# A two-layer long-convolution and SwiGLU kernel: a new hand-written order, searched with another charge for a held GpSimd instruction

## The chip, the cores and the metric

The kernel runs on one core of one Trainium2 chip. The metric is the device time of one execution in microseconds, as the median of several runs. The engines are named as in the profile: PE (TensorE), with PEld its weight loads, DVE (VectorE), ACT (ScalarE), POOL (GpSimd) and SP (SyncE, which here only issues transfers).

## The reference

Two layers, each a gated long convolution with a residual, and then a SwiGLU feed-forward block with a residual, on 2048 rows of 512 columns in bf16. Both layers use the same weights.

```python
x = A_q                                              # 2048 x 512
for layer in (0, 1):                                 # written out twice in the reference
    x = x + conv_block(layernorm(x), A_k, A_v, A_shift_k, A_ssm_k, A_ssm_D)
    x = x + ffn(layernorm(x), B_w_gate, B_w_up, B_w_down)

def conv_block(q, k, v, shift_k, ssm_k, ssm_D):
    k_shift = sum over 4 taps t of k shifted down by 3 - t rows, times shift_k[:, 3 - t]
    kv = k_shift * v
    y = irfft(rfft(kv padded to 4096) * rfft(ssm_k padded to 4096))[:2048]
    return q * (y + kv * ssm_D)

def ffn(x, w_gate, w_up, w_down):                    # 512 -> 1792 -> 512
    return (silu(x @ w_gate) * (x @ w_up)) @ w_down
```

The convolution's result y depends only on k, v and the filter, so both layers use the same y, and only the layer norms, the products with q and the feed-forward blocks differ between them.

## The kernel before, in words

The rows are cut into four chunks of 512 rows (NB = 4) and each chunk into two halves of 256 rows. A half in one layer is a unit (layer, chunk, half). The convolution is done chunk by chunk as matmuls with cosine and sine tables (`fwd` and `inv`): the spectra X (of kv) and G, H (of the filter) come out of TensorE into PSUM, are evicted to SBUF mostly by ScalarE, are multiplied on VectorE (tiles `t`, `Z`, `m`), and go through TensorE again to give `Yk`.

A unit's feed-forward block takes the normalised rows, transposed as `zT` (by a transposing transfer from SyncE's queue, for the first half by TensorE), multiplies them with the gate and up weights into PSUM tiles `pf`, which ScalarE evicts (`sg` with silu, `hr` or `ht` as a copy); VectorE multiplies the two; in groups handled by rows the product `hr` is transposed by a transfer into `sg`, and TensorE multiplies it with the down weights into `pd`. Some groups use a seven-product scheme instead (`cb`, `ps7`, evicted as `mt`).

A layer norm takes the mean and variance of a row either on VectorE (`bn_stats`, `bn_aggr` into `mv`, columns of constants in `bst` appended) or on ScalarE (sums by `jk`, with `nm` and then `ve`), and then needs (variance + eps) to the power -0.5. That power is a tiny GpSimd instruction, 128 x 2 elements, written to `rstd` (`power`, line 905 of the profile): after `mv` or after `ve`. VectorE or ScalarE then normalises with `rstd`, in some cases through `nmr` = -mean * rstd.

Every piece of work is registered with `add` as an operation with its engine, a cost, and its reads and writes: 1716 operations, of which 523 are TensorE's, 488 ScalarE's, 512 VectorE's, 150 SyncE's and 43 GpSimd's. `ORDER` is a table of 1716 ranks: the nth number is the place of the nth registered operation in one global list. `Plan.order` sorts by it and `Plan.walk` goes through the list with a timing model, which chooses the slot of each ring buffer. `Plan.issue` then emits the operations in the list's order. Each engine therefore executes its own operations in the list's order, and waits across engines are made by semaphores that follow from the reads and writes. The model's times are not on the chip; what reaches it are the order on each engine, the ring slots, and where the fixed number of 33 warm-up matmuls go at the start.

In the model a power whose input ports are taken by VectorE is held: `pend` is the pending power and `held` the time until which VectorE's back-to-back SBUF-to-SBUF operations keep it. It is settled when an operation that needs it is reached, when VectorE leaves a hole, or when the next GpSimd operation in the list is reached.

The operations that the steps below touch are: `ve` (operation 107), the first power (108), `nmr` (109), the two memsets of `bst` (2 and 3, lines 1276 and 1277), the squares `jk` (105 and 106), the evictions of X (line 525, operations 132, 135, 116, 119, 147, 141, 138, 144), the products `t` and `Z` (lines 748 and 752), the first normalised `z` (line 964) and the transfers into `zT` (line 994) and `sg` (line 1132).

Of the kernel before, what the change touches and what calls it, by code (L numbers as in the profile page):

```python
# [149 lines left out]
class Plan:  # L150
# [79 lines left out]
    def walk(self, seq, loads):  # L230
# [6 lines left out]
        def settle(g):  # L237
            pend.end = max(pend.start + pend.cost, g + pend.cost - 0.08)
            t["POOL"] = max(t["POOL"], pend.end)
# [1289 lines left out]
```

## Time and profile before

| what | before |
|---|---|
| median of 3 runs | 339.8 us (339.25 to 340.37) |
| the profiled execution's own time | 339.51 us |
| its span, first to last instruction | 337.7 us |
| granted TensorE clock | 1.00 |
| PE busy | 330.9 us, 98% |
| DVE busy | 299.9 us, 89% |
| ACT busy | 262.8 us, 78% |
| POOL busy | 35.4 us, 10%, in 48 instructions |

Matmuls are pipelined and their ends are modelled, so a busy PE is not PE at its peak, and a few per cent of the matmuls' records are missing (2141 matmuls against 2172 weight loads). In an answer of the timeline a row gives start, duration, engine, line, operation, tiles, count, and in brackets the idle time of the engine just before it with what ended it. In an answer of the waits a row gives the waiting instruction, what it waited for, the total in us, the number of times and the longest. The time outside the span (1.8 us) has no instruction in it.

### The profile page before, as it was taken

Reading aid. Unit: us, or ns where it says so; the run is one execution under the profiler, and the core shown is the slowest. Engines: PE = TensorE matmul, PEld = TensorE weight load, DVE = VectorE, ACT = ScalarE, POOL = GpSimd, SP = SyncE. Lnnn points to the kernel's source line nnn. Section 1 sums busy time; section 2 is a strip of 40 time slices with the busy share of each in tenths; the row PEclk is TensorE's granted clock in tenths of the full one; section 3 lists DMA queues with packets and bytes.
Section 4 is the critical chain, followed back from the end, with each engine's and each line's share of the span. In section 5 each row is a group of like instructions: output and inputs, shape, how many; then the busy total and the mean of one; then the engine's idle time right before and its main releaser. Section 6 shows DMA issues by size and latency. Waiting matters only on the chain.

```text
span 337.7 us, 5898 instructions
## 1 busy us (share of the span) xinstructions
PE 330.9 (98%) x2141; PEld 204.6 (61%) x2172; DVE 299.9 (89%) x512; ACT 262.8 (78%) x534; POOL 35.4 (10%) x48
## 2 busy tenths in 40 slices
PE   9999999999999999999999999999999999999996
PEld 7655864645445564745454464744455687858884
DVE  8899999999888998999999999999999787877545
ACT  7889999999967466999899894999675556475462
POOL 4050001102100000122010100011100100100000
PEclk9999999999999999999999999999999999999999
DMA  7999604632346147421324434510514230204101
GB/s 255 350 229 376 130 13 66 151 82 41 71 93 94 36 91 188 95 49 32 62 53 106 97 60 110 138 35 16 96 28 82 56 72 17 48 18 93 49 3 62
DMA packets 77993, 31.59 MB, mean 94 GB/s; under 512 B 69766, under 2 KB 75787, under 8 KB 77963
## 3 DMA queue, kind: packets, MB, share of 16 engines
q1 hardware_dynamic: 77808, 31.13, 39.6%
q8 instruction: 17, 0.28, 0.4%
q14 instruction: 14, 0.11, 0.1%
q10 hardware_dynamic: 154, 0.07, 0.1%
HBM read 12.33 MB, written 2.10 MB: 43 GB/s over the span
## 4 chain that ended last, share of the span: by engine, by line
PE 91%; ACT 4%; DMA 2%; issue 1%; DVE 1%; SPq 1%
PE pf L416 56%; PE pd L1210 20%; PE ps L1085 7%; PE ps L416 6%; DMA kTb<-in_A_k_dram 1%; PE wm L1495 1%; DMA sg<-hr 1%; ACT H L525 1%; SPq L1132 1%; ACT ks L620 1%; ACT n L959 0%; ACT jk L929 0%; DVE t L748 0%; ACT ev L525 0%; ACT hr L1124 0%
## 5 line engine op out<-in xcount | busy, mean ns | idle before, releaser
L416 PEld LDWEIGHTS <-zT 128*128 128x128 bf16 x528 | 51.6, 98 | 58.5 <-DMA zT<-z 0.2
L416 PE MATMUL pf<-wg_sb,zT 128*128 128x512 bf16 x255 | 64.3, 379 | 0.5
L416 PE MATMUL pf<-wu_sb,zT 128*128 128x512 bf16 x260 | 64.3, 379 | 0.2
L1210 PE MATMUL pd<-wd_sb,sg 128*128 128x512 bf16 x189 | 48.1, 379 | 0.9 <-DMA sg<-hr 0.3
L1124 ACT CAST hr<-pf 128x512 bf16<-128x512 f32 x66 | 38.4, 593 | 12.4 <-PE pf L416 8.5
L1123 ACT ACTIVATE sg<-pf 128x512 bf16<-128x512 f32 x66 | 38.8, 608 | 11.3 <-PE pf L416 10.2
L416 PE MATMUL pf<-zT,wg_sb 128*128 128x256 bf16 x368 | 46.0, 273 | 0.1
L416 PE MATMUL pf<-zT,wu_sb 128*128 128x256 bf16 x368 | 45.9, 273 | 0.0
L758 DVE TENSOR_TENSOR t<-X,G 128x4096 bf16<-128x4096 bf16 x18 | 40.9, 2284 | 0.1
L416 PEld LDWEIGHTS <-wu_sb 128*128 128x128 bf16 x368 | 36.0, 98 | 8.1
L416 PEld LDWEIGHTS <-wg_sb 128*128 128x128 bf16 x368 | 35.9, 98 | 7.9 <-issue 0.4
L1183 ACT ACTIVATE sg<-pf 128x512 bf16<-128x512 f32 x46 | 27.3, 607 | 10.8 <-PE pf L416 10.8
L1187 ACT CAST ht<-pf 128x512 bf16<-128x512 f32 x46 | 26.8, 595 | 9.8 <-PE pf L416 8.0
L905 POOL TENSOR_TENSOR rstd<-mv,nhalf 128x2 f32<-128x2 f32 x20 | 17.0, 852 | 158.2 <-DVE mv L915 134.7
L1210 PEld LDWEIGHTS <-sg 128*128 128x128 bf16 x200 | 19.5, 98 | 21.7 <-DMA sg<-hr 0.8
L1210 PE MATMUL pd<-wd_sb,ht 128*128 128x512 bf16 (+1 forms) x124 | 29.7, 369 | 0.1
L914 DVE BATCH_NORM_STATS2 bst<-xc 128x6 f32<-128x512 bf16 x40 | 26.5, 683 | 0.5
L905 POOL TENSOR_TENSOR rstd<-ve,nhalf 128x2 f32<-128x2 f32 x12 | 14.6, 1218 | 111.7 <-ACT ve L942 111.7
L1190 DVE TENSOR_TENSOR ht<-ht,sg 128x512 bf16<-128x512 bf16 (+1 forms) x31 | 16.6, 544 | 8.8 <-ACT sg L1183 4.5
L1130 DVE TENSOR_TENSOR hr<-hr,sg 128x1024 bf16<-128x1024 bf16 x27 | 18.4, 682 | 4.2 <-ACT sg L1123 2.0
L1210 PEld LDWEIGHTS <-ht 128*128 128x128 bf16 x126 | 12.3, 98 | 13.1 <-DVE ht L1190 0.3
L525 ACT ACTIVATE X<-ps 128x512 bf16<-128x512 f32 x32 | 18.4, 604 | 1.6 <-PE ps L416 0.9
(143 smaller groups left out, 522.1 us busy)
## 6 DMA issues: line engine op xcount, KB each, us to landing
hn<-in_A_ssm_k_dram SPq DMA_DIRECT2D x4, 512.0 KB, 3.7
vt<-in_A_v_dram SPq DMA_DIRECT2D x4, 512.0 KB, 5.5
xc<-in_A_q_dram SPq DMA_DIRECT2D x4, 512.0 KB, 5.6
out_dram<-xc SPq DMA_DIRECT2D x15, 128.0 KB, 1.9
wg_sb<-in_B_w_gate_dram SPq DMA_DIRECT2D x1, 1792.0 KB
wu_sb<-in_B_w_up_dram SPq DMA_DIRECT2D x1, 1792.0 KB, 8.9
wd_sb<-in_B_w_down_dram SPq DMA_DIRECT2D x1, 1280.0 KB, 12.1
sg<-hr SPq DMA_TRANSPOSE x66, 2.4
```

The costliest lines, as they stand in the source:

```text
L416: nc.tensor.matmul(o, lhsT=lhsT, rhs=rhs, start=(n == 0), stop=(n == len(terms) - 1))
L525: add("ACT", act(D), lambda: nc.scalar.activation(out=view(), in_=ps.t[:], func=ACT.Copy, scale=scale), r=[ps], w=[(buf, keys)], conv=conv)
L758: dve(8 * D, lambda t=t, part=part: nc.vector.tensor_mul(out=t.t[:], in0=x.t[:, :, part:part + 1, :].to_broadcast((P, R, 2, D)), in1=g.t[: ...
L905: add("POOL", cost, lambda: nc.gpsimd.tensor_tensor(out=rstd.t[:], in0=var(), in1=nhalf.t[:].to_broadcast((P, n)), op=ALU.pow), r=reads + ...
L914: add("DVE", 0.6, lambda st=st, i=i: nc.vector.bn_stats(out=st.t[:, 0:6], in_=xs[c].t[:, i, :]), r=[(xs[c], (i,))], w=[st])
L1085: nc.tensor.matmul(bank.t[:, half_ * C:(half_ + 1) * C], lhsT=lhsT(i), rhs=rhs(i), start=(first and i == 0 and half_ == 0), stop=(last and ...
L1123: add("ACT", act(D), lambda ps=ps, dst=dst, o=o, which=which: nc.scalar.activation(out=rows(dst, o), in_=ps.t[:], func=ACT.Silu) if which ...
L1124: out=rows(dst, o), in_=ps.t[:], func=ACT.Silu) if which == "g" else nc.scalar.copy(out=rows(dst, o), in_=ps.t[:]),
L1130: dve(n * W, lambda: nc.vector.tensor_mul(out=hr.t[:], in0=hr.t[:], in1=sg.t[:]), [sg], [hr], due=(unit, k / pairs, 0.0, "h"))
L1183: add("ACT", act(D), lambda ps=ps, o=o, sg=sg: nc.scalar.activation(out=sg.t[:, o:o + 2, :], in_=ps.t[:], func=ACT.Silu), r=[ps], w=[(sg, ...
L1187: add("ACT", act(D), lambda ps=ps, o=o, ht=ht: nc.scalar.copy(out=ht.t[:, o:o + 2, :], in_=ps.t[:]), r=[ps], w=[(ht, (o // 2,))], due=(uni ...
L1210: nc.tensor.matmul((pds[o] if not cs.start else pds[HP]).t[:, cs], lhsT=ht.tiles(q, o), rhs=wt["d"].t[:, ft, cs], start=(ft == std0 and no ...
```

## The change

Two things change: one constant of the timing model in `walk`, and the whole table `ORDER`, which was searched anew with that constant. No operation is added, removed or altered.

```diff
 ORDER = [
-    7, 79, 141, 188, 2, 3, 1, 15, 23, 4, 12, 0, 5, 13, 68, 9, 10, 6, 8, 11, 28, 19, 14, 24, 20, 25, 32, 33, 38, 69, 144, 146, 18, 46, 17, 45, 22, 43,
...
+    10, 40, 110, 214, 1, 6, 7, 8, 21, 2, 3, 0, 4, 5, 14, 12, 9, 11, 13, 16, 24, 20, 17, 22, 23, 26, 28, 31, 34, 15, 45, 50, 27, 43, 19, 47, 37, 44,
...
 ]
...
             if pend is not None and (o.eng == "POOL" or pend in o.preds):
-                settle(held if pend.late == 1 or pend in o.preds else max(held, pend.start) + 1.2)
+                settle(held if pend.late == 1 or pend in o.preds else max(held, pend.start) + 4.0)
                 pend = None
```

Read as ranks, the operations of the first layer norm and around it move so:

| operation | rank before | rank after |
|---|---|---|
| memset of bst, first (2) | 141 | 110 |
| memset of bst, second (3) | 188 | 214 |
| second square, jk (106) | 124 | 111 |
| first two X evictions (132, 135) | 111, 117 | 116, 120 |
| ve (107) | 133 | 124 |
| next X evictions (116, 119, 138) | 119, 121, 126 | 126, 129, 151 |
| power, rstd (108) | 134 | 170 |
| last Z product ahead of nmr | 163 (158) | 169 (159) |
| nmr (109) | 165 | 171 |
| first kTb product of the next chunk | 166 (259) | 167 (253) |
| ks evictions (260, 254) | 171, 206 | 183, 191 |

126 rows, old and new, of the table ORDER are left out of this document.

## Prediction

> **What bounds the kernel now.** I read the page first: busy time, clock and the chain that ended last.
>
> ```profile
> span 337.7 us, 5898 instructions
> PE 330.9 (98%) x2141; PEld 204.6 (61%) x2172; DVE 299.9 (89%) x512; ACT 262.8 (78%) x534; POOL 35.4 (10%) x48
> PEclk9999999999999999999999999999999999999999
> PE 91%; ACT 4%; DMA 2%; issue 1%; DVE 1%; SPq 1%
> ```
>
> TensorE is busy for 330.9 of 337.7 us at a full clock, and it carries 91% of the chain. The change leaves every matmul in place; it only moves them. So a new order can win no more than the time in which TensorE stands, and the next view is who TensorE waited for, and then its timeline around those waits.
>
> ```profile
> PE ps L416 <- DMA kTb<-in_A_k_dram: 0.8, 1, 0.8
> PE pd L1210 <- DMA sg<-hr: 0.3, 1, 0.3
> PE ps L416 <- ACT ks L620: 0.2, 1, 0.2
> ...
> 183.88 4.32 PE pf L416 x20
> ...
> 22.76 1.08 PE L416 MATMUL ps<-dg,kTb 128*128 128x128 bf16 x16 [0.82 <-DMA kTb<-in_A_k_dram]
> ...
> 31.27 0.38 PE L416 MATMUL ps<-vt,fwd 128*128 128x512 bf16 x1 [0.21 <-ACT ks L620]
> 31.55 0.72 PE L1022 MATMUL ptz<-ident,z 128*128 128x128 bf16 x8
> 32.33 0.59 PE L416 MATMUL ps<-vt,fwd 128*128 128x512 bf16 x2
> 32.88 0.49 PE L416 MATMUL pf<-zT,wg_sb 128*128 128x256 bf16 x3
> ...
> 241.33 1.04 PE L1210 MATMUL pd<-wd_sb,sg 128*128 128x512 bf16 x4 [0.33 <-DMA sg<-hr]
> 333.19 1.47 PE L1210 MATMUL pd<-wd_sb,ht 128*128 128x256 bf16 x12
> ```
>
> Twenty 512-column matmuls take 4.32 us, so one costs 0.216 us of TensorE's time, although a single one is drawn 0.38 long; a stall is therefore 0.16 us longer than its bracket. Read so, TensorE lost 0.98 us before 22.76 (0.82 + 0.16), 0.37 at 31.27 (0.21 + 0.16), and 0.49 at 241.33 (0.33 + 0.16). From 31.27 to 32.88 pass 1.61 us for three vt matmuls, one whose record is missing (0.86 together) and eight transposes of z at about 0.056: 0.3 lost there too. After 333.19 + 1.47 = 334.66 there is only the tail, to 337.7. Between 32.88 and 334.66 only the 0.49 us is lost: the whole body is full. The pool to win from is 0.98 + 0.37 + 0.3 + 0.49 = 2.1 us, 0.6% of the time; what can be lost is open.
>
> The head (to 32.88) is where the altered charge belongs, so I read VectorE and GpSimd there.
>
> ```profile
> 15.64 1.28 DVE L748 TENSOR_TENSOR t<-X,G 128x1024 bf16<-128x1024 bf16 x2
> 16.96 0.43 DVE L752 TENSOR_TENSOR Z<-t,t 128x512 bf16<-128x512 bf16 x1
> ...
> 20.15 4.36 POOL L905 TENSOR_TENSOR rstd<-ve,nhalf 128x2 f32<-128x2 f32 x1 [13.43 <-ACT ve L942]
> 24.47 0.11 POOL L1276 MEMSET bst<- 128x12 f32 x1
> ...
> 22.52 1.42 DVE L752 TENSOR_TENSOR Z<-t,t 128x512 bf16<-128x512 bf16 x4
> 24.55 0.16 DVE L953 TENSOR_TENSOR nmr<-nm,rstd 128x2 f32<-128x2 f32 x1 [0.61 <-POOL rstd L905]
> 24.63 1.89 DVE L889 TENSOR_TENSOR m<-Z 128x1024 bf16<-128x1024 bf16 x3
> 31.08 0.73 DVE L964 TENSOR_SCALAR z<-xc,mv,rstd 128x512 bf16<-128x512 bf16 x2 [0.25 <-POOL rstd L905]
> ...
> 56.84 0.68 DVE L663 TENSOR_TENSOR X<-m 128x1024 bf16<-128x1024 bf16 x1
> 57.53 0.69 DVE L1130 TENSOR_TENSOR hr<-hr,sg 128x1024 bf16<-128x1024 bf16 x1
> 57.10 0.97 POOL L905 TENSOR_TENSOR rstd<-ve,nhalf 128x2 f32<-128x2 f32 x1 [9.77 <-ACT ve L942]
> 191.46 1.23 POOL L905 TENSOR_TENSOR rstd<-ve,nhalf 128x2 f32<-128x2 f32 x1 [17.00 <-ACT ve L942]
> ```
>
> The first power (rstd of L905) took 4.36 us where others take 0.97 or 1.23. It starts at 20.15 while VectorE runs SBUF-to-SBUF operations without a break, and ends 0.57 after the last of them (22.52 + 1.42 = 23.94). It is also the only one with an unrelated GpSimd instruction, the bst memset, queued behind it. VectorE then idles 0.61 us for it, and from 24.55 VectorE works through to z at 31.08 nearly without a hole. So that 0.61 us sits on the path that sets 32.88.
>
> **The change part by part.** The constant is not on the chip; what changes is the order of each engine and the ring slots. Reading each list position of the two tables as the rank of that operation: of TensorE's 523 entries 445 stand elsewhere, of ScalarE's 488 it is 415, of VectorE's 512 it is 390, of SyncE's 150 it is 105, of GpSimd's 43 it is 16. Costs of the instructions stay, so each goes in at zero by itself; the sum is of waits.
>
> *The first power.* Before, ScalarE computes ve after five X evictions, both squares and the hs copy; after, it comes right after the first two X evictions. One bst memset goes ahead of the power (rank 110 against 170), the other still stands next behind it (rank 214).
>
> ```profile
> 10.42 0.60 ACT L525 ACTIVATE ev<-ps 128x512 bf16<-128x512 f32 x1 [0.67 <-PE ps L416]
> 13.31 1.09 ACT L525 ACTIVATE ev<-ps 128x512 bf16<-128x512 f32 x2 [0.35 <-PE ps L416]
> 14.98 1.08 ACT L525 ACTIVATE X<-ps 128x512 bf16<-128x512 f32 x2
> 16.33 0.60 ACT L525 ACTIVATE X<-ps 128x512 bf16<-128x512 f32 x1 [0.26 <-PE ps L564]
> 19.76 0.31 ACT L942 ACTIVATE ve<-sm,eps 128x2 f32<-128x2 f32 x1
> 23.88 0.59 ACT L620 CAST ks<-ps 128x512 bf16<-128x512 f32 x1 [0.78 <-PE ps L416]
> ```
>
> The second square is moved ahead of the X evictions; the holes of 0.67 and 0.35 us on ScalarE take most of its 0.81, because the table puts the ev matmuls ahead of the kTb ones. So the two X evictions stay at about 14.98, ve runs at 16.0 to 16.3 in a hole that was 0.26, and the power starts at 16.3 instead of 20.15. VectorE's order up to 16.96 is the same, and 14.98 leads to 15.64: at 15.64 + 1.28 = 16.92 it leaves a hole of 0.04 (Z at 16.96 needs the t just written). At 57.52/57.53 a hole of 0.01 was enough: that power ended at 58.07, 0.55 after it. I take it that 0.04 is enough too: rstd is ready near 17.5, seven microseconds before nmr needs it. nmr then follows the last Z without a hole, 0.08 ahead of its drawn end as the m at 24.63 is ahead of nmr's (24.71): 23.86 instead of 24.55, a gain of 0.69. The bounds are 0 (the hold lasts to 23.94 as before, since nmr stands behind the same products) and 0.7; the row at 57.10 is nearest, so 0.69. If ve comes later than 16.9 the cover is gone and the value is 0.
>
> The Trainium skill, page "SBUF — State Buffer", section "SBUF: two separate sides", says that VectorE and GpSimd hold the shared port pair as an exclusive lock for one whole instruction and the loser blocks. The trace agrees for 57.10 and 191.46, but not for 20.15, which was passed over for nine VectorE instructions. By that rule alone the power at 20.15 would have taken about what those two took, the old charge would do, and this part would be worth 0.
>
> *What else is late then.* z moves from 31.08 to about 30.4 if ScalarE and TensorE follow. ScalarE had a hole of 0.78 at 23.88; the table now puts three H evictions there and ks behind. TensorE gets three matmuls more ahead of the kTb ones (3 x 0.216 = 0.65 of the 0.98). One more vt product is put between z and the zT copy, which I take to cost 0.09 (of its 0.33 all but what TensorE's transposes cover). Head: 0.69 - 0.09 = 0.6, with bounds 0 and, if TensorE's stalls up to 32.88 all went, 1.6.
>
> *The body.* Here each hand-over by a transposing DMA is packed tightly, and re-packed by the new table. At 241.33 the distance in matmul time from the last product to its consumer was 5.2 us; in the new table the smallest such distance is 5.6. So the 0.49 there may go; but others shrink (rivals). I set the body's stalls equal, 0.49, bounds 0 and 2.8. *Tail:* the last four down-projection blocks stand in the same sequence, behind 1.7 us of filler for the last silu; 0, with 0.2 either way.
>
> Sum against the profiled execution: 339.5 (337.7 span + 1.8 around it) - 0.6 = 338.9. That execution lies 0.3 under the median of the runs, 339.8, so on the median's scale 339.2.
>
> **The rivals.** *Slower: a transpose that lands late.* The new table has less TensorE work between products and the layer norm's consumer at some units.
>
> ```profile
> 168.15 1.03 PE L416 MATMUL ps<-Z,inv 128*128 128x512 bf16 x4
> 179.15 2.50 SPq L994 DMA_TRANSPOSE zT<-z  x2
> 183.71 1.46 PE L416 MATMUL pf<-wg_sb,zT 128*128 128x512 bf16 x6
> 278.63 0.71 PE L1085 MATMUL ps<-wsa,cb 128*128 128x256 bf16 x5
> 294.67 1.19 SPq L994 DMA_TRANSPOSE zT<-z  x1
> 299.30 1.03 PE L416 MATMUL pf<-wu_sb,zT 128*128 128x512 bf16 x4
> ...
> sg<-hr SPq DMA_TRANSPOSE x66, 2.4
> ```
>
> With 2.4 us from issue to landing, zT issued at 179.15 was there at 181.6 and used at 183.7: 2.1 spare. The tables cut the matmul time from the inverse's product (168.15) to that use from 15.1 to 12.3 us, 2.8 less: 0.7 short. For the one issued at 294.67 (297.1, used 299.3, 2.2 spare) the cut is from 20.1 to 16.7, 3.4 less: 1.2 short. TensorE takes its queue in order, so each shortfall moves the end. Both come to 1.9; with the 0.4 to 0.5 that the other shortened places would add, 2.3: 339.2 + 2.3 = 341.5. For it: those distances, and 0.49 at 241.33 shows that a miss costs what it is late. Against it: the same tables move VectorE and ScalarE work out from between (twelve strangers instead of fifteen on VectorE in the second). It decides the sign once the shortfalls left over exceed 1.6 us.
>
> *No effect at the power.* The memset of rank 214 has nothing to wait for, so it still stands behind the power on the chip; the planner escapes its charge because nmr precedes it in the list. If a follower makes the hold and a 0.04 hole isn't enough, VectorE idles 0.61 at 24.55 as now, and the rest is equal: 339.8.
>
> *Faster.* The head gains 0.6 and the hand-over at 241.33, with 5.6 or more everywhere, no longer stalls: 0.6 + 0.49 = 1.1, giving 338.7.
>
> **How the numbers follow.** A measurement of this kernel can tell about 0.3%, 1.0 us. Forecast (339.2) 0.35, no effect at the power (339.8) 0.10, faster (338.7) 0.24, slower (341.5) 0.31. Same is then 0.45. The range leaves out a full 2.1 us gain and a third late hand-over: 338.3 to 341.7.
>
> **What would show it.** Right: a first power that starts near 16.3 and lasts about 1.2 us, nmr with no idle time before it, the first pf matmul near 32.3, span near 337.1. Wrong in the head: a power of 4 us or more and 0.6 idle before nmr. Wrong in the body: TensorE waits on zT<-z or sg<-hr of more than 0.5 in all between 33 and 334. The prediction fails if those waits exceed 2.5 us, or if the X evictions slip past 15.5 because ScalarE's holes do not take the square.

## The result and the profile after

| | before | after |
|---|---|---|
| median of 18 runs each | 339.57 us (339.25 to 340.37) | 340.56 us (339.83 to 342.45) |
| ratio to before, 95% interval | | 1.0033 [1.0021, 1.0045] |
| profiled execution, its span | 339.51 us, 337.7 us | 341.35 us, 339.6 us |

The new order is slower, by about 1 us, and its runs scatter more (2.6 us from lowest to highest, 1.1 before). The profiled execution of after lies 0.8 us above its median, so its terms are larger than the median's. In one execution, the profiled one of E1, the granted TensorE clock was 0.85 and the time 389.31 us; it enters no ratio, and no view below is of it. The page of after, busy time and chain:

```profile
span 339.6 us, 5922 instructions
PE 334.0 (98%) x2172; PEld 203.9 (60%) x2172; DVE 299.6 (88%) x512; ACT 262.9 (77%) x534; POOL 34.1 (10%) x48
PE 87%; DMA 5%; DVE 4%; SPq 1%; issue 1%; ACT 0%
PE pf L416 54%; PE pd L1210 20%; PE ps L1085 7%; PE ps L416 6%; DMA xc<-in_A_q_dram 4%; DMA kn<-in_A_k_dram 1%; SPq L460 1%; DVE G L687 1%; DVE m L646 1%; DVE t L758 1%; DVE bst L914 1%; DVE H L652 0%; DVE ht L1190 0%; ACT ev L525 0%; SPq L500 0%
```

TensorE's share of the chain fell from 91% to 87%, and 4% now runs through a load, xc<-in_A_q_dram, that the chain of before did not show. The first power and what follows it, from the timeline of after:

```profile
16.09 1.29 DVE L748 TENSOR_TENSOR t<-X,G 128x1024 bf16<-128x1024 bf16 x2
16.79 1.17 POOL L905 TENSOR_TENSOR rstd<-ve,nhalf 128x2 f32<-128x2 f32 x1 [9.79 <-ACT ve L942]
17.41 0.42 DVE L752 TENSOR_TENSOR Z<-t,t 128x512 bf16<-128x512 bf16 x1
...
24.32 0.15 DVE L953 TENSOR_TENSOR nmr<-nm,rstd 128x2 f32<-128x2 f32 x1
32.64 1.03 PE L416 MATMUL pf<-zT,wu_sb 128*128 128x256 bf16 x8
33.51 1.04 PE L416 MATMUL pf<-zT,wg_sb 128*128 128x256 bf16 x8
...
334.62 1.90 PE L1210 MATMUL pd<-wd_sb,ht 128*128 128x512 bf16 x14
```

The power lasts 1.17 us instead of 4.36 and nmr has no idle time before it. From the first t to nmr pass 24.32 - 16.09 = 8.23 us, before 24.55 - 15.64 = 8.91. The first pf matmul is at 32.64 against 32.88. The last group of matmuls ends at 334.62 + 1.90 = 336.52 against 334.66. So the head is 0.24 us shorter, the body 303.88 long against 301.78, 2.10 longer, and the tail the same (3.1 against 3.0). Where the body lost it, first TensorE and ScalarE, then VectorE, from the same timeline:

```profile
42.46 0.38 PE L416 MATMUL ps<-vt,fwd 128*128 128x512 bf16 x1
43.66 1.04 PE L1210 MATMUL pd<-wd_sb,ht 128*128 128x512 bf16 x4 [0.83 <-DVE ht L1190]
45.09 1.03 PE L416 MATMUL pf<-zT,wg_sb 128*128 128x256 bf16 x8 [0.39 <-ACT sg L1183]
45.96 1.04 PE L416 MATMUL pf<-zT,wu_sb 128*128 128x256 bf16 x8
47.03 0.38 PE L416 MATMUL ps<-vt,fwd 128*128 128x512 bf16 x1
...
48.98 0.38 PE L416 MATMUL ps<-vt,fwd 128*128 128x512 bf16 x1
49.52 1.69 PE L1210 MATMUL pd<-wd_sb,ht 128*128 128x512 bf16 x7 [0.16 <-DVE ht L1190]
...
43.04 1.52 ACT L959 ACTIVATE n<-xc,nmr,rstd 128x512 bf16<-128x512 bf16 x2 [1.95 <-DVE nmr L953]
...
32.07 0.42 DVE L1025 COPY zT<-ptz 128x512 bf16<-128x512 bf16 x1
34.98 0.69 DVE L914 BATCH_NORM_STATS2 bst<-xc 128x6 f32<-128x512 bf16 x1 [2.49 <-DMA xc<-in_A_q_dram]
35.59 2.34 DVE L646 TENSOR_TENSOR m<-H 128x2048 bf16<-128x2048 bf16 x2
...
42.92 0.69 DVE L1190 TENSOR_TENSOR ht<-ht,sg 128x1024 bf16<-128x1024 bf16 x1
```

At 0.216 us a 512-column matmul and 0.109 a 256-column one (32.64 to the next group at 33.51 is eight of them), TensorE stood 43.66 - 42.46 - 0.22 = 0.98, then 45.09 - 43.66 - 0.86 = 0.57, 47.03 - 45.96 - 0.87 = 0.20 and 49.52 - 48.98 - 0.22 = 0.32: 2.07 us. The small gaps further on come to 0.45 us and stand against the 0.49 that before lost at 241.33, so these four are nearly all of the body's loss. Each goes back to one place: VectorE stands 2.49 us at the batch-norm statistics of the xc row of chunk 1, which wait for the row's load, and everything behind it comes late: the products of the filter spectrum (m, H, G), nmr, for which ScalarE waits 1.95, and ht at 42.92. The answering rows of before:

```profile
32.31 0.42 DVE L1025 COPY zT<-ptz 128x512 bf16<-128x512 bf16 x1 [0.16 <-PE ptz L1022]
32.65 2.35 DVE L646 TENSOR_TENSOR m<-H 128x2048 bf16<-128x2048 bf16 x2
...
38.71 0.69 DVE L914 BATCH_NORM_STATS2 bst<-xc 128x6 f32<-128x512 bf16 x1
...
40.51 0.68 DVE L1190 TENSOR_TENSOR ht<-ht,sg 128x1024 bf16<-128x1024 bf16 x1
```

There the statistics stood behind the two m, four H and one G product. The load moved too. SyncE's queue in the timeline of before, and the load's row in the DMA view of that stretch (the last column is the time from issue to landing):

```profile
20.41 0.58 SPq L503 DMA_DIRECT2D wu_sb<-in_B_w_up_dram  x1
21.04 0.51 SPq L500 DMA_DIRECT2D wd_sb<-in_B_w_down_dram  x1
21.59 4.26 SPq L492 DMA_DIRECT2D xc<-in_A_q_dram  x1
25.89 0.43 SPq L500 DMA_DIRECT2D wd_sb<-in_B_w_down_dram  x1
```

```profile
xc<-in_A_q_dram SPq DMA_DIRECT2D x1, 512.0 KB, 12.8
```

The same two views of after:

```profile
19.67 0.58 SPq L503 DMA_DIRECT2D wu_sb<-in_B_w_up_dram  x1
20.30 1.13 SPq L500 DMA_DIRECT2D wd_sb<-in_B_w_down_dram  x2
21.47 4.74 SPq L492 DMA_DIRECT2D xc<-in_A_q_dram  x1
```

```profile
xc<-in_A_q_dram SPq DMA_DIRECT2D x1, 512.0 KB, 13.5
```

In after both parts of wd (512 KB and 1280 KB) go ahead of xc, in before only the larger one. Counted from the issue of wu, xc lands 21.59 + 12.8 - 20.41 = 14.0 us later in before and 21.47 + 13.5 - 19.67 = 15.3 in after. So two moves met: the load 1.3 us later in its queue, and its reader 6.3 us earlier on VectorE (38.71 to 32.4).

### The profile page after: what moved, and what is told of

Its sections match the earlier page's. It is cut to its first block, busy times and chain, and to the rows that moved or that the text cites. A ratio compares the mean times of both kernels' runs of the same rounds, so it can differ in the third digit from the quotient of the medians.

```text
span 339.6 us, 5922 instructions
## 1 busy us (share of the span) xinstructions
PE 334.0 (98%) x2172; PEld 203.9 (60%) x2172; DVE 299.6 (88%) x512; ACT 262.9 (77%) x534; POOL 34.1 (10%) x48
## 4 chain that ended last, share of the span: by engine, by line
PE 87%; DMA 5%; DVE 4%; SPq 1%; issue 1%; ACT 0%
PE pf L416 54%; PE pd L1210 20%; PE ps L1085 7%; PE ps L416 6%; DMA xc<-in_A_q_dram 4%; DMA kn<-in_A_k_dram 1%; SPq L460 1%; DVE G L687 1%; DVE m L646 1%; DVE t L758 1%; DVE bst L914 1%; DVE H L652 0%; DVE ht L1190 0%; ACT ev L525 0%; SPq L500 0%
## 5 line engine op out<-in xcount | busy, mean ns | idle before, releaser
L1210 PE MATMUL pd<-wd_sb,sg 128*128 128x512 bf16 x200 | 49.1, 379 | 0.0
L1123 ACT ACTIVATE sg<-pf 128x512 bf16<-128x512 f32 x66 | 38.2, 600 | 13.2 <-PE pf L416 10.8
L416 PE MATMUL pf<-zT,wg_sb 128*128 128x256 bf16 x368 | 46.7, 273 | 0.4 <-ACT sg L1183 0.4
L905 POOL TENSOR_TENSOR rstd<-mv,nhalf 128x2 f32<-128x2 f32 x20 | 18.2, 908 | 157.1 <-DVE mv L915 157.1
L1183 ACT ACTIVATE sg<-pf 128x512 bf16<-128x512 f32 x46 | 26.7, 603 | 8.2 <-PE pf L416 6.8
L905 POOL TENSOR_TENSOR rstd<-ve,nhalf 128x2 f32<-128x2 f32 x12 | 12.1, 1004 | 115.9 <-ACT ve L942 115.9
## 6 DMA issues: line engine op xcount, KB each, us to landing
wd_sb<-in_B_w_down_dram SPq DMA_DIRECT2D x1, 1280.0 KB, 12.8
```

Source lines behind the costliest of these rows:

```text
L416: nc.tensor.matmul(o, lhsT=lhsT, rhs=rhs, start=(n == 0), stop=(n == len(terms) - 1))
L905: add("POOL", cost, lambda: nc.gpsimd.tensor_tensor(out=rstd.t[:], in0=var(), in1=nhalf.t[:].to_broadcast((P, n)), op=ALU.pow), r=reads + ...
L1123: add("ACT", act(D), lambda ps=ps, dst=dst, o=o, which=which: nc.scalar.activation(out=rows(dst, o), in_=ps.t[:], func=ACT.Silu) if which ...
L1183: add("ACT", act(D), lambda ps=ps, o=o, sg=sg: nc.scalar.activation(out=sg.t[:, o:o + 2, :], in_=ps.t[:], func=ACT.Silu), r=[ps], w=[(sg, ...
L1210: nc.tensor.matmul((pds[o] if not cs.start else pds[HP]).t[:, cs], lhsT=ht.tiles(q, o), rhs=wt["d"].t[:, ft, cs], start=(ft == std0 and no ...
```

## The experiments

Theory T puts the loss on VectorE's early reader; R1 on the moved load alone; R2 on the head; R3 on the rest of the new order. All kernels were run beside the kernel before on the same chip, and the ratio is to that. The edits move entries of `ORDER` (E9 also lifts one dependence), and the diffs show one engine's sequence each, with the operation's number in brackets.

**E1: the reader back in its place.**

```diff
 VectorE, kernel after
   zT<-ptz (222)
-  bst<-xc (520)
   m<-H x2, H<-m x4, G<-H,G (251)
+  bst<-xc (520)
   G<-H,G (252)
```

> The kernel after, with one VectorE instruction put back: the batch-norm statistics (bst<-xc) that read the xc row of chunk 1 stand behind the first G product (H,G->G) again, as in the kernel before, instead of right behind the zT copy. Theory T (VectorE stands 2.49 us at that instruction for a load that lands at 34.97, and TensorE loses 2.06 us between 42.5 and 49.5 for it): no wait on xc on VectorE, TensorE stalls between 42 and 50 below 0.5 us, a median 1.0 to 2.0 us below that of after, so near 339.0 where after gave 340.56. Rival R1 (the SyncE move alone, xc issued behind all of wd, is the cost): no change, 340.6. Rival R3 (the loss is spread over re-packed hand-overs): less than 0.5 us gained, the stalls turn up elsewhere.

338.94 us, ratio 0.9985 [0.9976, 0.9994]. One instruction moved takes away the whole loss and some more: T's figure, 339.0, and not R3's; the order of the head (R2) is untouched by this edit. R1 predicted no change and falls in this form. The signs that T named for the profile are there in E10, which has the reader in the same place: no VectorE wait on xc, and no gap on TensorE between 42 and 50 us.

**E2: the load back in its place.**

```diff
 SyncE, kernel after
   wu (79)
-  wd, 512 KB (80)
   wd, 1280 KB (81)
   xc (287)
+  wd, 512 KB (80)
   vt (290)
```

> The kernel after, with one SyncE entry put back: the xc load of chunk 1 goes ahead of the 512 KB part of wd, as in before. VectorE's order is that of after. Theory T: xc lands about 0.6 us sooner (34.4 rather than 34.97), VectorE waits about 1.9 us instead of 2.49, and the median falls by 0.3 to 0.6 us, to about 340.1. R1: the whole loss goes, 339.0 to 339.3. R3: no change.

338.91 us, ratio 0.9981 [0.9972, 0.9990]. T had said 340.1, which was wrong: this move alone also takes the whole loss away. The waits between 31 and 52 us show why:

```profile
DVE bst L914 <- DMA xc<-in_A_q_dram: 0.6, 1, 0.6
```

Issued behind only the larger part, xc landed 13.9 us after the issue of wu; and in this execution wu went out at 18.94 rather than 19.67. VectorE waited 0.56 us, and of that 0.12 reached TensorE (a gap at 47.4). So some 0.4 us of the wait had cover here: what stood behind it could come that much later before TensorE had to stand. R1, which said 339.0 to 339.3 here, gets this one nearly right. So neither fits both runs, and the theory had to be: either move alone fits under the cover, both together do not (theory C).

**E3 and E4: each move alone, in the kernel before.**

```diff
 E3, VectorE, kernel before              E4, SyncE, kernel before
   zT<-ptz (222)                           wu (79)
+  bst<-xc (520)                        +  wd, 512 KB (80)
   m<-H x2, H<-m x4, G<-H,G (251)          wd, 1280 KB (81)
-  bst<-xc (520)                           xc (287)
   G<-H,G (252)                         -  wd, 512 KB (80)
```

> The kernel before, with one VectorE instruction moved: the batch-norm statistics of chunk 1's xc row stand right behind the zT copy, ahead of the products of the filter spectrum, as in after. Theory T: VectorE waits 34.4 - 32.65 = about 1.8 us for xc there, everything behind it is late by that, TensorE stalls 1 to 1.8 us between 40 and 50, median 340.6 to 341.3 where before gave 339.57, with a wider spread. R1 and R3: no change beyond 0.3 us.

> The kernel before, with one SyncE entry moved: the xc load of chunk 1 goes behind both parts of wd, as in after. Theory T: xc lands 0.6 us later or so, about 35.0, and the statistics that read it run at 38.7 as before, so no change: 339.4 to 339.8. R1: 1 us slower or more, 340.6.

E3: 340.02 us (339.41 to 341.27), ratio 1.0010 [0.9999, 1.0021]; E4: 339.77 us, 1.0003 [0.9994, 1.0012]. E4 came as T expected. E3 is at most half of what T expected, and its interval takes in no change. In its profiled execution VectorE waited 0.26 us for xc, since xc landed at 33.36 rather than 34.4, and TensorE lost 0.3 behind it, in three gaps of 0.1 that before does not have. The first of them, 43.39 - 42.41 - 0.87 = 0.11:

```profile
42.41 1.04 PE L416 MATMUL pf<-zT,wg_sb 128*128 128x256 bf16 x8
43.39 1.03 PE L416 MATMUL pf<-zT,wu_sb 128*128 128x256 bf16 x8
```

The others are at 44.36 and 48.15. That fits the 0.4 by which the median lies above that of before.

**E5 and E6: none of the two moves in after, both in before.** E5 has the edits of E1 and E2, E6 those of E3 and E4.

> The kernel after, with both places put back: the statistics of chunk 1's xc row behind the first G product, and the xc load ahead of the 512 KB part of wd. Theory C (the loss is a conjunction: moved behind wd, xc lands 15.0 to 15.3 us after the issue of wu instead of 13.9, and moved ahead of the filter products, its reader waits for it; either one put back removes it): no more than either repair alone gave, 338.9 within 0.2, lowest spread of all, no VectorE wait on xc. Rival: the two costs add, then this gains again about 0.6, 338.3.

> The kernel before, with both moves made, the statistics early and the xc load behind all of wd, and nothing else of the change. Theory C: xc lands 15.2 us after the issue of wu, which came between 18.5 and 20.4, so at 33.7 to 35.6, VectorE reaches its reader at about 32.65 and waits 1.1 to 3.0 us; some 0.5 of it is hidden, the rest reaches TensorE: median 340.3 to 341.2 where the single moves gave 340.02 and 339.77. Rival R3 (the rest of the new order is needed for the loss): no more than the two single moves together, 340.2 or less, and no TensorE stall over 0.3 us between 40 and 50.

E5: 338.95 us (338.68 to 339.33), ratio 0.9980 [0.9972, 0.9989]. E6: 341.0 us (five executions), 1.0043 [1.0030, 1.0055]. Theory C holds on both sides. In before the two moves cost 0.4 and 0.2 us singly, neither clear of the scatter, and 1.4 together; in after they cost nothing singly and 1.6 together (340.56 against 338.95). The waits of E6 between 31 and 52 us are those of after, smaller:

```profile
ACT n L959 <- DVE nmr L953: 1.1, 1, 1.1
DVE bst L914 <- DMA xc<-in_A_q_dram: 1.0, 1, 1.0
```

Its timeline has the loss on TensorE, eight 256-column matmuls and then a gap:

```profile
42.60 1.04 PE L416 MATMUL pf<-zT,wg_sb 128*128 128x256 bf16 x8
44.37 1.03 PE L416 MATMUL pf<-zT,wu_sb 128*128 128x256 bf16 x8 [0.74 <-ACT sg L1183]
```

That gap is 44.37 - 42.60 - 0.87 = 0.90; with two of 0.1 at 45.34 and 49.13 TensorE lost 1.1 us, all of VectorE's 1.04. The VectorE wait and TensorE's loss behind it in the profiled executions are 0.26 and 0.3 (E3), 1.04 and 1.1 (E6) in the order of before, and 0.56 and 0.12 (E2), 2.49 and 2.07 (after) in the new one: in these executions the order of before pays the wait in full, and the new one hides some 0.4 us of it. What in the new order hides them is not shown.

**E9: the early reader with an early load.** VectorE's order is the change's own.

```diff
 SyncE, kernel after
   wu (79)
+  xc (287)
   wd, 512 KB (80)
   wd, 1280 KB (81)
-  xc (287)
 line 1461
-        load_x(c, after=[wd])
+        load_x(c, after=[wu if c == 1 else wd])
```

> The kernel after with VectorE's order as the change has it (statistics of chunk 1's xc row right behind the zT copy), but the xc load directly behind wu, ahead of both parts of wd. In the profiles a 512 KB part ahead of xc delayed its landing by 1.3 us (13.9 to 15.2 after the issue of wu), so 1792 KB less ahead should bring it to about 10.6 after the issue of wu, 29 to 31. Theory C: VectorE, there at 32.3, waits for nothing, TensorE has no stall over 0.3 between 40 and 50, median 338.7 to 339.0, a spread under 1 us: the early place of the statistics costs nothing by itself. Rival (the early statistics cost by holding the filter products up by their own 0.7 us, or wd, landing later, stalls the down-projection at 42): 339.4 or more.

338.86 us, ratio 0.9981 [0.9972, 0.9991]. xc landed 9.6 us after its issue at 19.17, that is 10.2 after the issue of wu, 5.1 sooner than in after. The early place of the statistics costs nothing in this order; only the landing counts. E1, E2, E5, E9 and E10 lie within 0.1 us of one another, and each beats both kernels, before by 0.15 to 0.2%, and after, going by the medians, by 0.5%.

**E7: no GpSimd instruction behind the power.** The altered charge is for a power with a follower, so this takes the follower away.

```diff
 GpSimd, kernel before
+  bst memset (2)
+  bst memset (3)
   rstd<-ve,nhalf (108)
-  bst memset (2)
-  bst memset (3)
```

> The kernel before, with the two bst memsets of GpSimd moved ahead of the first power, so that no other GpSimd instruction stands behind it. It tests what the altered charge says: that a GpSimd instruction that follows holds a power up. Theory F (the follower holds it): the power at 20.2 lasts 1 to 1.3 us instead of 4.36, nmr loses its 0.6 us of idle time, median 339.0. Theory H (only a hole between VectorE's instructions lets it in, follower or not): 4.36 us again, nmr waits 0.6, median 339.4 to 339.8.

339.65 us, ratio 1.0001 [0.9991, 1.0012]. The power and nmr:

```profile
20.95 4.37 POOL L905 TENSOR_TENSOR rstd<-ve,nhalf 128x2 f32<-128x2 f32 x1 [14.14 <-ACT ve L942]
25.35 0.16 DVE L953 TENSOR_TENSOR nmr<-nm,rstd 128x2 f32<-128x2 f32 x1 [0.61 <-POOL rstd L905]
```

Without any follower it lasts 4.37 us, as with it. Theory F falls; the follower does not hold the power.

**E8: only the early power, in before.**

```diff
 ScalarE, kernel before
+  square jk (106)
   X evictions (132, 135)
+  ve (107)
   X evictions (116, 119)
-  square jk (106)
   X eviction (138), hs copy (165)
-  ve (107)
```

> The kernel before, with two ScalarE instructions moved: the second square of the head ahead of the X evictions and ve right behind the first two of them, as in after; everything else as in before, the memsets behind the power too. Prediction's step for the first power: the power starts at 16.3 to 16.8, is let in by the hole of 0.04 us at 16.9, lasts about 1.2, nmr follows the last Z without idle time, gain 0.6, median 339.0. Rival: the X evictions slip by up to 0.8 us behind the square and eat the gain, 339.6.

340.01 us, ratio 1.0012 [1.0003, 1.0020]: slower. The first t of VectorE, the power and nmr:

```profile
17.17 1.29 DVE L748 TENSOR_TENSOR t<-X,G 128x1024 bf16<-128x1024 bf16 x2 [0.73 <-ACT X L525]
17.89 1.15 POOL L905 TENSOR_TENSOR rstd<-ve,nhalf 128x2 f32<-128x2 f32 x1 [11.16 <-ACT ve L942]
25.39 0.16 DVE L953 TENSOR_TENSOR nmr<-nm,rstd 128x2 f32<-128x2 f32 x1
```

The power lasts 1.15 us and nmr does not wait, but the square ahead of the evictions makes VectorE wait 0.73 for X, more than the 0.61 that nmr gave back. That is the rival's case, but the median lies 0.4 above that of before, and this difference gives only 0.1 of it; the rest is not shown. The change has the early power without this price, since in its order the first square runs at 12.55, ahead of two ev evictions, and the second at 14.73, about where before has its first.

**E10 and E11: the power later, in the repaired kernel E5.** ve goes behind the first four X evictions (E10) or behind the hs copy, as in before (E11).

> The repaired kernel (after with statistics and xc load both back in their places), with ve moved on ScalarE from behind the first two X evictions to behind the first four, so that the first power starts after VectorE's hole of 0.04 us at 17.5 to 17.7 instead of before it. Theory H (the power gets in only at a hole of VectorE): it starts near 18.5 and is held to 25.0, 5 us or more, nmr waits 0.6 us, median 0.4 to 0.7 us above the repaired kernel's 338.95, so 339.4 to 339.6. Rival (what matters is which instructions run beside it, a power started at 18.5 takes 1.2 us): no wait before nmr, 338.95.

> The repaired kernel (after with statistics and xc load both back in their places), with ve on ScalarE as late as in before, behind the hs copy, so that the first power starts near 21.2, beside t, m, t, t and four Z of VectorE. Theory Q (a power that starts while a queue of VectorE instructions stands ready is passed over by all of them): it is held to the last Z and 0.58 us beyond, to about 25.2, so it lasts some 4 us, nmr waits 0.6 us, and the median is 0.4 to 0.7 us above the repaired kernel's 338.95, near 339.5. Theory O (it only waits for the instruction that is running, wherever it starts, as at 18.76): 0.6 to 1.3 us, no wait, 338.9.

E10: 338.87 us, ratio 0.9981 [0.9972, 0.9989]; E11: 339.71 us, 0.9999 [0.9989, 1.0009]. The timeline of E10, then of E11:

```profile
18.01 1.29 DVE L748 TENSOR_TENSOR t<-X,G 128x1024 bf16<-128x1024 bf16 x2
18.76 1.11 POOL L905 TENSOR_TENSOR rstd<-ve,nhalf 128x2 f32<-128x2 f32 x1 [11.80 <-ACT ve L942]
19.21 1.09 DVE L752 TENSOR_TENSOR Z<-t,t 128x512 bf16<-128x512 bf16 x3
24.57 0.15 DVE L953 TENSOR_TENSOR nmr<-nm,rstd 128x2 f32<-128x2 f32 x1
```

```profile
21.01 0.69 DVE L889 TENSOR_TENSOR m<-Z 128x1024 bf16<-128x1024 bf16 x1
21.05 3.77 POOL L905 TENSOR_TENSOR rstd<-ve,nhalf 128x2 f32<-128x2 f32 x1 [14.03 <-ACT ve L942]
22.81 1.43 DVE L752 TENSOR_TENSOR Z<-t,t 128x512 bf16<-128x512 bf16 x4
24.85 0.16 DVE L953 TENSOR_TENSOR nmr<-nm,rstd 128x2 f32<-128x2 f32 x1 [0.61 <-POOL rstd L905]
```

E10 refutes theory H: VectorE goes from t to Z without a hole (18.01 + 1.29 = 19.30, Z at 19.21), and the power still ends at 19.87, 0.57 us behind the t that ran when it started. In E11 it starts at 21.05, is passed over by seven VectorE instructions and ends 0.58 us behind the last of them (22.81 + 1.43 = 24.24, against 24.82). That brings the 0.61 us before nmr back and costs 0.76 us in the median against E5, or 0.65 by the two ratios, as the kernel before gave 339.62 beside E5 and 339.76 beside E11.

**E12: which instruction stands beside it.**

```diff
 VectorE, kernel before
   t<-X,G (157)
-  m<-Z (184)
   t<-X,G x3, Z<-t,t x4, nmr (109)
+  m<-Z (184)
   m<-Z x3
```

> The kernel before, with the one m product of VectorE that runs when the first power starts (m<-Z at 20.11) moved behind nmr, to the other three; the power then starts beside t, t, t and four Z. Theory M (the hold comes from the power starting in the m product): the power lasts 1.2 us or less. Theory Q (any ready queue passes it over): it is held to the last Z again, 4.36 - 0.6 = 3.8 us, nmr 0.6 us behind the last Z. The time of the whole says little here, as the first inverse matmuls have to wait for m: 339.5 to 340.6.

339.42 us, ratio 0.9991 [0.9982, 1.0000]. The power lasted 0.72 us. But without m VectorE came to the next t too soon and stood 0.41 us for X, and the power ran in that hole; so M and Q are not told apart.

## Why the prediction was wrong

The forecast was 339.2 us, 0.6 below the 339.8 of the first three runs. It came out as 340.56, 1.0 above the 339.57 of 18 runs: the head gained what was forecast, and the body, set at no change, lost more.

*The first power: right in size, and in part by luck.* It gave 0.69 for VectorE's gain up to nmr; 8.91 - 8.23 is 0.68. The start came at 16.79 rather than 16.3, and the head's gain in the profile is 0.24 rather than 0.6 only because the chain began 0.45 us later in this execution (first t at 16.09 against 15.64); in the chain's own time the first pf came 16.55 us after the first t instead of 17.24. That start is the execution's and not the order's: in E9, which keeps the new head, the first t is at 15.68, in E7, which keeps the old one, at 16.43. E11 put a price on the hold in the whole time, 0.65 to 0.76 us. But the reason given, a hole of 0.04 us that lets the power in before 16.9, was not needed: in E10 a start at 18.76 was as good, and in E11 one at 21.05 was held. E7 shows that the follower, which the changed constant charges for, plays no part. The power at 20.15 was passed over by eight VectorE instructions, the m that ran when it started among them, and not by nine.

*The step that failed is the one before the sum: "Costs of the instructions stay, so each goes in at zero by itself", with the body's stalls then set equal.* SyncE's 105 and VectorE's 390 moved entries were counted and not walked. Only the hand-overs by transposing DMA were measured for their slack; no load was set against its reader. The rows of before had it, as shown above: xc lands at 34.4 and its reader comes at 38.71, 4.3 us of slack. The tables put the reader behind the zT copy, which ends at 32.7, and 512 KB more ahead of the load; the 1.3 us for those is measured, and the profile of before gives 1.4, as its DMA engines moved a mean of 373 GB/s from 26 to 34 us. That is a wait of 34.4 + 1.3 - 32.7 = 3.0 us on VectorE, a loss of up to that, where the sum had 0. It measured 2.49 and 2.07 in the profile, where wu went out 0.74 us earlier than in before, and 1.6 in the medians (340.56 against 338.95 of E5). The prediction's signs of being wrong in the body were waits on zT and sg of more than 0.5 us in all; those did not come, and a wait for a load was not among them.

*The slower rival had the sign and the wrong place.* It named two transposes, at 183.7 and 299.3. TensorE waits for neither in after: the gaps between its matmuls behind 49.52 come to 0.45 us, near 88, at 243 and at 278. *The faster rival's second half is half right:* the stall at 241.33 is not gone but halved, in after and in E5:

```profile
242.01 2.10 PE L1210 MATMUL pd<-wd_sb,sg 128*128 128x512 bf16 x8
243.95 1.03 PE L416 MATMUL pf<-wg_sb,zT 128*128 128x512 bf16 x4
```

```profile
239.99 2.15 PE L1210 MATMUL pd<-wd_sb,sg 128*128 128x512 bf16 x8
241.97 1.03 PE L416 MATMUL pf<-wg_sb,zT 128*128 128x512 bf16 x4
```

In after 243.95 - 242.01 - 8 x 0.216 = 0.21, in E5 241.97 - 239.99 - 8 x 0.216 = 0.25, instead of 0.49. With the two moves taken back the order gains 0.67 us, 338.95 against 339.62; the forecast had 0.6 and the faster rival 1.1.

*The median and the wider scatter.* In the profiled executions of before, of after and of E2 to E12 wu goes out between 18.55 and 20.41 us, behind the transposing loads of inv and kTb, and the landing of xc moves with it: where only the larger part of wd went ahead, it came between 32.4 (E5) and 34.4 (before). Where the reader stands within the cover this doesn't show (338.68 to 339.33 in E5); in after it would. That this makes the scatter of after is argued, not shown. Argued too is why the search put the reader there: the plan charges 10.5 us for the load of this row (line 492), and from issue to landing it took 12.4 to 13.7 wherever wd's larger part went ahead.

The Trainium skill, page "DMA: Bandwidth & Descriptors", section "Queues, rings and completion order", says that each DMA engine takes a ring's descriptors in the order in which they were put there. The traces agree: 512 KB more ahead on the same queue put xc's landing off by 1.3 us, 1792 KB less brought it forward by 5.1.

## What to carry to other kernels

When an order is searched anew, walk every queue and pair each load with its first reader: landing time, counted from the issue of the queue's burst, against the time at which the reader's engine gets there. Two moves that are each free can cost when they eat the same slack from its two ends, and taking one alone misleads: in the new kernel undoing either removes the whole loss and makes that move look like the only culprit, in the old kernel making either shows next to nothing. Run the four corners. An instruction that waits for a load holds up all that stands behind it on its engine, so a reader with nobody waiting for it belongs behind the work that others need.

## What the runs showed of the hardware

The hold of a GpSimd power is neither a matter of the next GpSimd instruction (4.37 us without one, E7) nor of a hole on VectorE (1.11 us without a hole, E10). It was let in at the end of the running VectorE instruction at 16.79, 17.89 (E8) and 18.76, and passed over by seven or eight at 20.15, 20.95 and 21.05. The Trainium skill, page "SBUF — State Buffer", section "SBUF: two separate sides", gives the shared port to whichever side starts first, for one whole instruction; the first three agree with that, the last three do not. What tells them apart is open. The held ones started 0.04 to 0.05 us behind the start of an m product, the others 0.09 to 0.16 behind that of a t; but a power at 191.46 of before, which started with a product (H), took 1.23 us, so a start that close does not make the hold by itself. E3, E4 and E6, with the head of before, show the same hold, and E2, E5 and E9, with that of after, none.
